# Thirteen identity matmuls put ahead of TensorE's first work, in a kernel whose order a planner writes

## The chip, the core and the metric

The kernel runs on one core of a Trainium2 chip. Its time is device time in microseconds (us), of one execution of the whole program; lower is better. Five engines run beside each other, each through its own list of instructions in the order in which they were issued: TensorE (in the profile PE for the matmuls and PEld for its weight loads), VectorE (DVE), ScalarE (ACT), GpSimd (POOL) and SyncE (SP, which here issues the DMAs). A span is the time from the first to the last instruction of one profiled execution.

## What is computed

First a chunked attention over `q`, `k`, `v` of shape (4, 8, 768, 64): each chunk of 32 queries sees 16 keys to the left, its own 32, 8 to the right, and 8 memory keys. Then a gated feed-forward network (FFN) on the 512-wide result.

```python
scores = scale * q_c @ k_full.T                 # per chunk of 32 queries
a = exp(scores - max); a = a / (sum(a) + 1e-9)
x = a @ v_full                                  # -> (4, 768, 512)

h = maximum(x @ w_in, 0)                        # 512 -> 1024
conv = cw[0]*h[t-1] + cw[1]*h[t] + cw[2]*h[t+1] # along the sequence, per channel
out = (h * 1/(1 + exp(-conv))) @ w_out          # 1024 -> 512
```

The weights `w_in`, `conv_w` and `w_out` arrive as float64. The kernel takes their 64-bit words apart on the chip and makes two single-precision parts of each (hi and lo), and it splits the activations in the same way, so each product of the FFN is three matmuls: hi·hi, hi·lo, lo·hi.

## The kernel before, in words

The attention is cut into 32 steps, numbered 0 to 31: four batches, two halves of the sequence, four pairs of heads. One step is:

- scores: 12 small matmuls on PE (L481, tile `s`);
- softmax: maximum on DVE (L397), exponential on ACT (L423 straight from the scores, or L402 on DVE and L435 on ACT), sum (L448) and reciprocal (L455) on DVE, the division on DVE or POOL (L459);
- three transposes on PE (L502, tile `t`), two copies of them on ACT into `a_d` (L513);
- 12 matmuls with the values on PE (L521, tile `a`), then the split of the result into `x_hi` on ACT (L530) and `x_lo` on DVE (L533).

The FFN takes 128 channels (one `fc` of eight) at a time. Its first layer (L556, 256 pieces of three matmuls) needs `x` of a half batch; ACT applies the ReLU (L573). The gate (L583 to L614) runs on ACT, DVE and POOL: three convolution taps (L583, L593), the sigmoid on ACT (L597), the product (L601), and the split into `g_hi` on ACT (L611) and `g_lo` (L614). The second layer (L632, 200 pieces of three matmuls) takes `g`; ACT copies the result out (L644), SP writes it. The conversions of the weights (L286 to L363) run on ACT, DVE and POOL during the first 115 us or so.

Exponential and sigmoid stand in two different function tables of ACT. Where the order goes from the one to the other, an ACT_TABLE_LOAD stands in the list of ACT.

The order of all this is not written by hand. Every piece of work is put down with `plan.op`: its engine, an assumed cost in ns, a due time from the table `DUE`, what it reads and writes, and for ACT which function table it needs. `Plan.run` then plays the whole program through with the assumed costs. At each moment it takes the engine that can start something earliest, and of what that engine could start within 1 ns the piece with the lowest due time; a piece that needs the other function table counts as 100.2 later (`SWITCH`). It also hands out the buffers: PSUM banks for `s` (2), `t` (1), `a` (1) and `f` (4, the FFN's), and the rings in SBUF. The engines' lists come out in the order in which the planner started the pieces, and on the chip each engine follows its list in that order, waiting wherever the next instruction's inputs are not there.

So the assumed cost of one piece does not only stand for itself: it sets when the planner thinks the engine is free, and with that the order of whatever comes after.

The identity (`ident`, 128x128, float32) is made at the start on POOL; the transposes use it.

Of the kernel before, what the change touches and what calls it, by code (L numbers as in the profile page):

```python
# [210 lines left out]


PAIRS = False
SWITCH, MODE = 100.2, 12.1


@with_exitstack
def attention_then_gated_ffn(
# [10 lines left out]
    nc = tc.nc  # L229
# [4 lines left out]
    P = 128  # L234
# [8 lines left out]
    plan = Plan()  # L243

    def tile_of(tag, n, shape, dtype=F32, pool=None):

        plan.ring(tag, n)
        pool = pool or work
        return Tile(tag, lambda: pool.tile(shape, dtype, name=tag, tag=tag, bufs=n))

    def bank(tag, n):
        return tile_of(tag, n, [P, 512], pool=psum)

    ident = const.tile([P, P], F32, name="ident")
# [117 lines left out]
    def attention(steps, due, soft, norm, zadd):  # L372
# [3 lines left out]
        W = 2 * NG * KW  # L376
        e = tile_of("e", 2, [P, 2, 2 * NG, KW]) if PAIRS else tile_of("e", 3, [P, 1, 2 * NG, KW])
        top, z = (tile_of(x, 4, [P, 2, 2 * NG]) for x in ("top", "z"))
# [198 lines left out]
    def gate(fc, h, due, tap, mult, keep=False):  # L577

        c = tile_of("c", 3, [P, S])
        w = [cw[:, 3 * fc + i : 3 * fc + i + 1] for i in range(3)]  # L580
        H = ((h, 0), (h, 1), "cw")
        if tap == "A":
            plan.op("A", act(S, ptr=1), due, lambda: nc.scalar.activation(c.t, h.t[:, 0:S], AF.Copy, scale=w[0]), H, (c,))  # L583
        else:
            plan.op(
                "V", vec(S, 2, 1), due,
                lambda: nc.vector.tensor_scalar(out=c.t, in0=h.t[:, 0:S], scalar1=w[0], scalar2=None, op0=ALU.mult),
                H, (c,), shared=True,
            )
        for i in (1, 2):  # L590
            plan.op(
                "V", vec(S, 1, 1), due,
                lambda i=i: nc.vector.scalar_tensor_tensor(  # L593
                    out=c.t, in0=h.t[:, i : i + S], scalar=w[i], in1=c.t, op0=ALU.mult, op1=ALU.add
                ), (*H, c), (c,), shared=True,
            )
        plan.op("A", act(S), due, lambda: nc.scalar.activation(c.t, c.t, AF.Sigmoid), (c,), (c,), table="sigmoid")  # L597
        y = (lambda: h.t[:, 1 : S + 1]) if keep else (lambda: c.t)
        plan.op(
            mult, vec(S) if mult == "V" else 2.0 * S, due,  # L600
            lambda: (nc.vector if mult == "V" else nc.gpsimd).tensor_tensor(  # L601
                out=y(), in0=c.t, in1=h.t[:, 1 : S + 1], op=ALU.mult
            ), (c, h), (h if keep else c,), shared=True,
        )
        return (h if keep else c), y
# [63 lines left out]
    def steps(i, n):  # L669

        while i < n:
            size = GROUP[i // 4] == "2" and i % 2 == 0 and 2 or 1
            attention(range(i, i + size), T_ATT[i : i + size], SOFT[i], NORM[i], ZADD[i])
            i += size

    def through_gate(b, fc, due, keep=False):
        i = b * NFC + fc
        return gate(fc, hs[b, fc][0], due, TAP[i], MULT[i], keep)

    steps(0, 4)  # L680
    for fc in range(NFC):
        convert("in", w_in[fc], w_in_p, fc, W_IN[fc], lin("w_in", fc), lin("w_in_load", fc))
# [8 lines left out]
    for fc in range(NFC):  # L691
        due = lin("gate0", fc)
        g.append(split(*through_gate(0, fc, due), due, LO[fc]))
# [4 lines left out]
    for tt in range(4, 6):  # L698
        ffn_out(0, g, tt, [lin("out0b", fc) + 0.1 * tt for fc in range(NFC)])
    y = [through_gate(1, fc, lin("gate1", fc), True) for fc in range(NFC)]  # L700
    g = [split(*y[fc], lin("split1", fc), LO[NFC + fc]) for fc in range(NFC)]
    steps(16, 24)
# [10 lines left out]
    for b in range(2, B):  # L713
        tokens_in(b, (0, 1), t, 4.2)
        g = []
        for fc in range(NFC):
            due = t + lin("gate", fc)
            g.append(split(*through_gate(b, fc, due), due, LO[b * NFC + fc]))
        if b + 1 < B:
            steps((b + 1) * NU, (b + 2) * NU)  # L720
        out_rest(b, g, t + 34, b + 1 == B)
        t += 34 + 34 + 14
# [78 lines left out]
```

## Time and profile before

| | |
|---|---|
| time, median of 3 runs | 358.87 us (358.48 to 359.29) |
| span of the profiled execution | 357.6 us |
| PE busy | 341.4 us, 95% of the span |
| DVE, ACT, POOL busy | 244.7, 240.4, 125.2 us |
| PE's first instruction | 6.8 us after the start |
| PE busy from 22.65 us to the end | 329.6 of 335.0 us |

The profiled execution is known by its span alone, 357.6 us; the median of the timed runs is 1.3 us above it, which is taken as what lies around the span. "Busy" is the time in which at least one instruction of the engine runs; instructions on PE overlap, so the durations of single ones add up to more than that.

### The profile page before, as it was taken

How to read it: one execution, taken by the hardware profiler on the slowest of the kernel's cores; microseconds unless marked ns; L12 is line 12 of the kernel's file. 1: busy time of each engine (PE TensorE's matmuls, PEld its weight loads, DVE VectorE, ACT ScalarE, POOL GpSimd, SP SyncE). 2: the span in 40 equal slices, each digit the busy share in tenths (PEclk: the TensorE clock that was granted, in tenths of full speed). 3: DMA queues.
4: the chain of work that ended last, by engine and by line, in shares of the span. 5: the costliest groups of instructions: out<-in, count | busy, mean ns of one | idle time of the engine just before them, and what ended most of it. 6: DMA issues, size and time to landing. Idle time of an engine off the chain costs nothing.

```text
span 357.6 us, 7589 instructions
## 1 busy us (share of the span) xinstructions
PE 341.4 (95%) x3000; PEld 302.1 (84%) x3000; DVE 244.7 (68%) x408; ACT 240.4 (67%) x492; POOL 125.2 (35%) x167
## 2 busy tenths in 40 slices
PE   1699999999999999999999999999999999999996
PEld 1588899999899987778888899997878799998886
DVE  3899898988889998779933026889644128998000
ACT  4468588878679999887979158877466345675101
POOL 2376554442373253774572003354010002560000
PEclk9989999999999999999999999999999999999999
DMA  7999961969623146134416200006272000000111
GB/s 267 402 387 311 383 234 63 341 208 283 209 95 116 25 139 227 68 104 152 129 44 250 88 31 0 2 0 188 80 294 75 30 31 2 0 0 3 59 59 61
DMA packets 19909, 48.63 MB, mean 136 GB/s; under 512 B 2337, under 2 KB 6689, under 8 KB 19873
## 3 DMA queue, kind: packets, MB, share of 16 engines
q1 hardware_dynamic: 19872, 48.14, 39.0%
q8 instruction: 24, 0.39, 0.5%
q14 instruction: 13, 0.10, 0.1%
HBM read 41.84 MB, written 6.29 MB: 135 GB/s over the span
## 4 chain that ended last, share of the span: by engine, by line
PE 69%; DVE 10%; DMA 5%; ACT 5%; POOL 5%; issue 4%; SPq 1%; POOLq 0%; DVEq 0%; ACTq 0%
PE f L632 33%; PE f L556 24%; PE a L521 5%; PE s L481 5%; DVE c L593 3%; PE t L502 2%; DMA h<-in_k_dram 2%; POOL c L601 2%; DMA w<-in_w_out_dram 2%; ACT c L597 2%; DMA w<-in_w_in_dram 2%; POOL w_top L293 2%; DVE z L448 1%; DVE w_top L299 1%; DVE top L397 1%
## 5 line engine op out<-in xcount | busy, mean ns | idle before, releaser
L632 PE MATMUL f<-w_out_hi,g 128*128 128x512 f32 (+1 forms) x400 | 127.6, 391 | 0.2 <-ACT o_sb L644 0.2
L556 PE MATMUL f<-x_hi,w_in_hi 128*128 128x384 f32 x256 | 88.7, 346 | 0.0
L632 PEld LDWEIGHTS f<-w_out_hi,g 128*128 128x128 f32 x400 | 74.1, 188 | 16.3 <-ACT o_sb L644 0.4
L556 PE MATMUL f<-x_hi,w_in_lo 128*128 128x384 f32 x256 | 86.2, 337 | 0.1
L556 PE MATMUL f<-x_lo,w_in_hi 128*128 128x384 f32 x256 | 86.1, 336 | 0.0
L593 DVE SCALAR_TENSOR_TENSOR c<-h,cw,c 128x768 f32<-128x768 f32 x48 | 65.9, 1380 | 27.6 <-ACT c L583 26.1
L632 PE MATMUL f<-w_out_lo,g 128*128 128x512 f32 (+1 forms) x200 | 77.0, 385 | 0.0
L556 PEld LDWEIGHTS f<-x_hi,w_in_hi 128*128 128x128 f32 x256 | 48.1, 188 | 1.2
L556 PEld LDWEIGHTS f<-x_hi,w_in_lo 128*128 128x128 f32 x256 | 48.2, 188 | 0.5 <-POOL w_in_lo L358 0.4
L556 PEld LDWEIGHTS f<-x_lo,w_in_hi 128*128 128x128 f32 x256 | 48.1, 188 | 0.0
L632 PEld LDWEIGHTS f<-w_out_lo,g 128*128 128x128 f32 x200 | 37.6, 188 | 7.2
L601 POOL TENSOR_TENSOR c<-c,h 128x768 f32<-128x768 f32 x9 | 15.8, 1752 | 70.2 <-ACT c L597 68.1
L459 POOL TENSOR_TENSOR e<-e,z 128x384 f32<-128x384 f32 x24 | 24.9, 1035 | 41.4 <-DVE z L455 27.1
L644 ACT COPY o_sb<-f 128x512 f32<-128x512 f32 (+1 forms) x25 | 14.1, 569 | 35.1 <-PE f L632 32.8
L573 ACT ACTIVATE h<-f 128x384 f32<-128x384 f32 x48 | 23.1, 492 | 17.2 <-PE f L556 16.8
L521 PEld LDWEIGHTS a<-a_d,v_t 128*64 128x64 f32 x768 | 25.7, 140 | 10.3 <-issue 5.0
L513 ACT COPY a_d<-t 64x384 f32<-64x384 f32 x64 | 30.3, 474 | 4.3 <-PE t L502 3.3
L533 DVE TENSOR_TENSOR x_lo<-a,x_hi 128x384 fp32r<-128x384 f32 x32 | 17.6, 551 | 22.3 <-ACT x_hi L530 22.2
L521 PE MATMUL a<-a_d,v_t 128*64 128x64 f32 x768 | 29.9, 229 | 1.9 <-ACT a_d L513 1.8
L597 ACT ACTIVATE c<-c 128x768 f32<-128x768 f32 x32 | 26.9, 845 | 3.8 <-DVE c L593 3.6
L530 ACT CAST x_hi<-a 128x384 fp32r<-128x384 f32 x32 | 15.4, 481 | 20.2 <-PE a L521 18.6
L423 ACT ACTIVATE e<-s,top 128x64 f32<-128x64 f32 (+3 forms) x96 | 24.4, 319 | 4.2 <-DVE top L409 2.8
(73 smaller groups left out, 479.8 us busy)
## 6 DMA issues: line engine op xcount, KB each, us to landing
v_t<-in_v_dram SPq DMA_DIRECT2D x32, 384.0 KB, 4.1
q_d<-in_q_dram SPq DMA_DIRECT2D x28, 384.0 KB, 5.1
k_t<-in_k_dram SPq DMA_DIRECT2D x28, 252.0 KB, 5.2
out_dram<-o_sb SPq DMA_DIRECT2D x23, 256.0 KB, 2.1
w<-in_w_in_dram SPq DMA_DIRECT2D x8, 512.0 KB, 5.9
w<-in_w_out_dram SPq DMA_DIRECT2D x8, 512.0 KB, 6.4
h<-in_q_dram SPq DMA_DIRECT2D x4, 384.0 KB, 7.0
h<-in_k_dram SPq DMA_DIRECT2D x4, 252.0 KB, 7.1
```

The lines of the kernel that those rows point to most:

```text
L423: nc.scalar.activation(part(e, i)[r, g, c], s_()[r, g, c], AF.Exp, bias=part(top, i)[r, g : g + 1], scale=SCALE, accum_out=part(z, i)[r, g ...
L459: lambda i=i: (nc.vector if norm == "V" else nc.gpsimd).tensor_tensor(out=part(e, i), in0=part(e, i), in1=part(z, i).unsqueeze(2).broadcas ...
L481: nc.tensor.matmul(s.t[j * D : (j + 1) * D, o : o + KW], lhsT=q_d.t[:, c], rhs=k_t.t[:, c * STEP : c * STEP + KW], start=True, stop=True,)
L513: nc.scalar.copy(out=a_d[r, :, p, :], in_=t.t[r, : NG * P].rearrange("p (g q) -> p g q", q=CH))
L521: nc.tensor.matmul(a.t[h * D : (h + 1) * D, g * P + j * D : g * P + (j + 1) * D], lhsT=v_t.t[:, g, j, h], rhs=a_d[:, 4 * g + 2 * j + h].re ...
L533: lambda: nc.vector.tensor_tensor(out=x_lo.t[:, cc], in0=a.t[:, :TW], in1=x_hi.t[:, cc].bitcast(F32), op=ALU.subtract),
L556: nc.tensor.matmul(f.t[:, :TW], lhsT=w_in_p[c][:, fc, cc], rhs=x_p[a].t[:, cc], start=(cc == 0 and i == 0), stop=(cc == NCC - 1 and i == 2),)
L573: nc.scalar.activation(h.t[:, 1 + o : 1 + o + TW], f.t[:, :TW], AF.Relu)
L593: lambda i=i: nc.vector.scalar_tensor_tensor(out=c.t, in0=h.t[:, i : i + S], scalar=w[i], in1=c.t, op0=ALU.mult, op1=ALU.add), (*H, c), (c ...
L597: plan.op("A", act(S), due, lambda: nc.scalar.activation(c.t, c.t, AF.Sigmoid), (c,), (c,), table="sigmoid")
L601: lambda: (nc.vector if mult == "V" else nc.gpsimd).tensor_tensor(out=y(), in0=c.t, in1=h.t[:, 1 : S + 1], op=ALU.mult), (c, h), (h if kee ...
L632: nc.tensor.matmul(ps.t[:, :n], lhsT=g[fc][a].t[:, tt * P : (tt + 1) * P], rhs=w_out_p[c][:, fc, o : o + n], start=(fc == 0 and i == 0), s ...
```

## The change

A constant `WARM = 13`, and one more piece of work ahead of all the others: 13 matmuls of the identity with itself, 128x128 by 128x128 in float32, into a bank of the FFN's ring `f` that nothing reads. It is put down for PE with a cost of 430 ns for each matmul, 5590 ns in all, and a due time of -1000, so the planner takes it first.

```diff
+WARM = 13
 SWITCH, MODE = 100.2, 12.1
...
+    def warm_up():
+        x = bank("f", 4)
+
+        def mm():
+            for _ in range(WARM):
+                nc.tensor.matmul(x.t[:, :P], lhsT=ident, rhs=ident, start=True, stop=True)
+
+        plan.op("PE", 430 * WARM, -1000, mm, (), (x,), mode="whole")
...
+    warm_up()
     steps(0, 4)
```

Nothing else in the text differs, and no piece of work is removed. The line numbers of the changed kernel are one higher from the constant to the function, 11 higher behind it.

The order does differ. The first place is the head of PE's list. Now:

```order
L682 MATMUL f<-ident 128x128 x13
L482 MATMUL s<-h 64x64 x48
L503 MATMUL t<-ident,e 128x128 x3
L522 MATMUL a<-a_d,v_t 64x64 x12
L503 MATMUL t<-ident,e 128x128 x3
L482 MATMUL s<-k_t,q_d 64x64 x12
L522 MATMUL a<-a_d,v_t 64x64 x12
```

Behind the 13 matmuls stand the same rows as before, the scores of steps 0 to 3 (x48) first. The lists of all engines go on unchanged for some time, PE's for 30 rows, DVE's for 45, ACT's for 23, POOL's for 25, SP's for 30; from there on they differ in many places.

The second place is the list of ACT between the exponential of step 12 and that of step 13. Before (the three rows of L423 are the exponential of step 13; `w_out_hi` is a converted weight, `c` and `g` belong to the gate and the FFN):

```order
L423 ACTIVATE e<-s,top 128x64 x6
L573 ACTIVATE g<-f 128x384 x3
L312 CAST w_out_hi<-w_top 128x512
L583 ACTIVATE c<-g,cw 128x768
L423 ACTIVATE e,z<-s,top 128x64 x5
L423 ACTIVATE e,z<-s,top 64x64
L423 ACTIVATE e,z<-s,top 64x56
L530 CAST x_hi_1111<-a 128x384
```

Now:

```order
L424 ACTIVATE e<-s,top 128x64 x6
L574 ACTIVATE g<-f 128x384 x3
L313 CAST w_out_hi<-w_top 128x512
L584 ACTIVATE c<-g,cw 128x768
L598 ACT_TABLE_LOAD
L598 ACTIVATE c<-c 128x768
L290 ACTIVATE w_top<-w_1055 128x512
L531 CAST x_hi_1118<-a 128x384
L574 ACTIVATE g<-f 128x384 x2
L612 CAST g<-c 128x768
```

A load of the sigmoid's table and a first sigmoid (L598) have come in where the exponential of step 13 stood. That exponential comes 33 rows further on, behind a load of the other table:

```order
L584 ACTIVATE c<-g,cw 128x768 x2
L313 CAST w_out_hi<-w_top 128x512
L574 ACTIVATE h<-f 128x384
L424 ACT_TABLE_LOAD
L424 ACTIVATE e,z<-s,top 128x64 x5
L424 ACTIVATE e,z<-s,top 64x64
L424 ACTIVATE e,z<-s,top 64x56
```

Before, ACT loaded no sigmoid table ahead of the exponentials of steps 13 to 16; now it does so once and loads the exponential's table back. The whole list has 18 table loads before and 18 now.

The third place is PE's list at the transposes of step 16. Now:

```order
L557 MATMUL f<-x_lo_1340,w_in_hi 128x384
L482 MATMUL s<-k_t,q_d 64x64 x24
L522 MATMUL a<-a_d,v_t 64x64 x12
L557 MATMUL f<-x_hi_1321,w_in_hi 128x384
L557 MATMUL f<-x_hi_1321,w_in_lo 128x384
L557 MATMUL f<-x_lo_1340,w_in_hi 128x384
L503 MATMUL t<-ident,e 128x128 x3
```

Here the scores of two steps (x24) and the values of step 15 stand close ahead of the transposes of step 16. Counted from the start of the list, 17 steps of scores and 106 pieces of the FFN's first layer stood ahead of these transposes before, and 20 steps of scores and 103 pieces do now; ahead of the values of step 16 it was 17 and 109, and is 20 and 108.

On DVE's list, ahead of the reciprocal of step 16, there are now two more multiply-adds of the gate (L593), two more products (L601) and one more split (L614) than before, and eight shorter instructions trade places, four for four. On ACT's list, ahead of the copies of `a_d` for step 16, there are now one exponential (L435), two first taps (L583), a sigmoid (L597), two casts of `g_hi` (L611) and two table loads more, and one ReLU (L573) less.

## The prediction

> **What bounds the kernel now.** I read the page's head and its chain first, then PE's busy time by stretches.
>
> ```profile
> span 357.6 us, 7589 instructions
> PE 341.4 (95%) x3000; PEld 302.1 (84%) x3000; DVE 244.7 (68%) x408; ACT 240.4 (67%) x492; POOL 125.2 (35%) x167
> PE 69%; DVE 10%; DMA 5%; ACT 5%; POOL 5%; issue 4%; SPq 1%; POOLq 0%; DVEq 0%; ACTq 0%
> ...
> 0.00:22.65 22.65, 11.72 (x178) 10.45 (x179) 15.61 (x39) 11.21 (x23) 9.72 (x17) 0.92 0.94 348
> 22.65:357.60 334.95, 329.63 (x2823) 291.63 (x2822) 229.06 (x370) 229.18 (x469) 115.50 (x151) 1.00 0.36 122
> 60.00:111.00 51.00, 50.23 (x549) 46.87 (x549) 44.55 (x87) 42.22 (x116) 21.14 (x39) 1.00 0.61 199
> ```
>
> In the stretches the columns are the length, then busy time of PE, PEld, DVE, ACT and POOL, then the granted clock. PE sets the end: from 22.65 us on it is idle for 334.95 - 329.63 = 5.3 us in all. PE's work is fixed, so an idle microsecond that is added there is added to the end, and one taken away at the start is taken away at the end, as long as its inputs keep up. Whether they do is read from 60 to 111 us: DVE is busy 44.55 and ACT 42.22 of 51 us, so those two can't fall far behind the order they have now.
>
> At the start, in order of time:
>
> ```profile
> 0.99 0.29 POOL masks.py:199 TENSOR_SCALAR_AFFINE_SELECT ident<-ident 128x128 f32<-128x128 f32 x1
> 6.82 1.55 PE L481 MATMUL s<-h 128*64 128x64 f32 x24 [6.82 <-DMA h<-in_k_dram]
> 8.41 0.56 DVE L397 TENSOR_REDUCE top<-s 128x6 f32<-128x384 f32 x1 [0.62 <-PE s L481]
> 10.09 4.77 PE L481 MATMUL s<-h 128*64 128x64 f32 x72 [1.72 <-DMA h<-in_k_dram]
> 14.90 0.75 PE L502 MATMUL t<-ident,e 128*128 128x128 f32 x3
> 17.48 0.92 PE L521 MATMUL a<-a_d,v_t 128*64 128x64 f32 x24 [1.82 <-ACT a_d L513]
> 19.27 1.55 PE L481 MATMUL s<-k_t,q_d 128*64 128x64 f32 x24 [0.40 <-DVE z L448]
> 20.58 1.52 PE L521 MATMUL a<-a_d,v_t 128*64 128x64 f32 x24
> 22.39 0.42 PE L556 MATMUL f<-x_hi,w_in_hi 128*128 128x384 f32 x1
> ...
> 18.00:19.00 1.00, 0.87 (x17) 0.56 (x13) 0.64 (x4) 0.98 (x3) 0.86 (x2) 0.89 1.06 401
> 19.00:20.00 1.00, 0.73 (x14) 0.76 (x16) 1.00 (x3) 0.95 (x4) 1.00 (x2) 0.50 1.08 405
> 22.00:23.00 1.00, 1.00 (x8) 0.81 (x6) 0.97 (x3) 0.75 (x2) 1.00 (x2) 0.90 1.02 403
> ```
>
> The scores of a step (x24) take 1.55 us where PE is slow; 24 matmuls of that shape take 0.92 us at 17.48. The slow ones at 19.27 and 20.58 coincide with a granted clock of 0.50. That from 6.82 the column shows 1.00 beside the same 1.55 us I take for a missing first record: PE starts at half clock.
>
> **The change, part by part.**
>
> *The thirteen matmuls.* They can start when the identity is there, at 0.99 + 0.29 = 1.28 us. PE's first work waits for its DMA until 6.82, and that wait is their cover. The trace has no plain float32 matmul of this shape. The scores are 12 in the program and 24 in the trace, so I count 26. Upper bound by the three transposes at 14.90, same shape at half clock: 26 x 0.25 = 6.5 us, end at 7.8, which is 1.0 late. Lower bound by the scores, half the columns: 26 x 0.065 = 1.7 us, end at 3.0. I take the end before 6.82: the clock should rise on the way. If the cover fails, step 0's scores end at 7.8 + 0.92 = 8.7 instead of 8.37: a loss of 0.3. Nobody waits for the bank that they write but later matmuls on PE itself.
>
> *A faster clock at the start.* Step 0's scores would end at 6.82 + 0.92 = 7.74 instead of 8.37, 0.63 us earlier, and DVE waited 0.62 us for them. Step 1's scores wait for their own DMA until 10.09 whatever the clock; if it holds, they too end 0.63 earlier. The scores and values at 19.27 and 20.58 could lose 0.6 us each. So the gain is at most 0.6 + 1.2 = 1.8 us and at least the loss of 0.3, if the clock falls again in the pause from 7.74 to 10.09. In the trace it did fall to 0.50 after a pause of 1.82 us (before 17.48). Since DVE is nearly full by then (1.00 and 0.97 of the last two rows), I take 0.5 us.
>
> [...]
>
> *The order.* This is the larger part. The planner keeps PE taken for 5.59 us more at the start, and from about the thirtieth row on all lists differ. What matters is the stretch before 111 us, where a sigmoid now stands ahead of the exponential of step 13. I compare what each engine must do before step 16, because there the trace shows almost no room:
>
> ```profile
> 107.56 0.82 POOL L459 TENSOR_TENSOR e<-e,z 128x384 f32<-128x384 f32 x1
> 108.49 0.50 PE L502 MATMUL t<-ident,e 128*128 128x128 f32 x3
> 109.61 0.95 ACT L513 COPY a_d<-t 64x384 f32<-64x384 f32 x2
> 110.61 0.49 PEld L521 LDWEIGHTS a<-a_d,v_t 128*64 128x64 f32 x14 [0.37 <-ACT a_d L513]
> ```
>
> The softmax ends at 108.38 and the transposes start at 108.49: 0.11 us of room. The copies end at 110.56, the values start at 110.61: 0.05. Prices, from the groups by form (busy, mean ns of one) and two pieces of the chain (start, us):
>
> ```profile
> L593 DVE SCALAR_TENSOR_TENSOR c<-g,cw,c 128x768 f32<-128x768 f32 x16 | 18.0, 1132 | 0.9 <-ACT c L583 0.8
> L601 DVE TENSOR_TENSOR c<-c,g 128x768 f32<-128x768 f32 x3 | 2.8, 951 | 0.0
> L614 DVE TENSOR_TENSOR g<-c,g 128x768 fp32r<-128x768 f32 x16 | 16.1, 1005 | 2.6 <-ACT g L611 2.5
> L597 ACT ACTIVATE c<-c 128x768 f32<-128x768 f32 x32 | 26.9, 845 | 3.8 <-DVE c L593 3.6
> L597 ACT ACT_TABLE_LOAD x9 | 11.5, 1283 | 0.1
> L583 ACT ACTIVATE c<-g,cw 128x768 f32<-128x768 f32 x8 | 7.5, 933 | 0.0
> L611 ACT CAST g<-c 128x768 fp32r<-128x768 f32 x24 | 20.0, 832 | 7.2 <-DVE c L601 4.4 <-POOL h L544 1.3 <-POOL c L601 1.2
> L435 ACT ACTIVATE e<-e 128x384 f32<-128x384 f32 x17 | 8.8, 522 | 2.9 <-DVE e L441 2.7
> L573 ACT ACTIVATE h<-f 128x384 f32<-128x384 f32 x48 | 23.1, 492 | 17.2 <-PE f L556 16.8
> ...
> 46.72 0.70 PE s L481 x24
> 112.23 10.10 PE f L556 x57
> ```
>
> So a step's scores cost PE 0.70 us and an FFN piece of three matmuls 10.10 / 19 = 0.53.
>
> - DVE, ahead of the reciprocal of step 16: 2 x 1.13 + 2 x 0.95 + 1.01 = 5.2 us more (of the eight short instructions that trade places four go and four come; counted as nothing). PE, ahead of the transposes: three scores more and three pieces less, 3 x 0.70 - 3 x 0.53 = 0.5. PE waits 5.2 - 0.5 - 0.1 = 4.6 us.
> - ACT, ahead of the copies: 0.52 + 2 x 0.93 + 2 x 1.28 + 0.85 + 2 x 0.83 - 0.49 = 7.0 us more. PE, ahead of the values: 3 x 0.70 - 0.53 = 1.6. PE waits 7.0 - 1.6 - 0.05 = 5.4 us.
>
> These two are one wait, not two: what delays the softmax delays the copies. It shrinks by what idle time DVE and ACT can fill, since PE is then the one that waits:
>
> ```profile
> DVE w L315 <- DMA w<-in_w_out_dram: 1.9, 1, 1.9
> DVE top L397 <- PE s L481: 1.4, 2, 0.9
> ...
> ACT x_hi L530 <- PE a L521: 1.7, 3, 0.8
> ACT g L573 <- PE f L556: 1.2, 3, 0.6
> ACT x_hi L530 <- PE f L556: 1.0, 1, 1.0
> ```
>
> These are waits between 60 and 111 us. Without its waits for PE, DVE's sum falls to 4.6 - 1.4 = 3.2, without the DMA's too to 1.3; ACT's falls to 5.4 - 3.9 = 1.5. Lower bound of the stall 1.3; upper bound 5.4, and 6.6 if the clock drops once on the way, as at 19.27 and 20.58 (0.6 us on each). I take 4.0, between 3.2 and 5.4: the wait for DMA has its own cause and may stay. Then steps 17 to 20 run with what they are given, and from step 21 on both orders have done nearly the same work, so nothing is added and nothing is won back: PE has no idle time left to fill.
>
> [...]
>
> *Sum*, against the profiled execution: 357.6 - 0.5 + 4.0 = 361.1 us of span, and 1.3 us around it (the median of the runs is 358.87): **362.4 us**. With the bounds together: 357.6 - 1.8 + 1.3 + 1.3 = 358.4, and 357.6 + 0.3 + 6.6 + 1.3 = 365.8.
>
> **The rivals.**
>
> *The start wins (0.16).* The clock holds through the pauses, 1.8 us are won, and DVE and ACT fill nearly all their idle time, which leaves 0.5 us of stall: 357.6 - 1.8 + 0.5 + 1.3 = 357.6 us. For it: the waits for PE between 60 and 111 us. Against it: DVE is 87% busy there, and its waits for PE are only 1.4 us. It decides from the point where the stall is below 1.8.
>
> *Even (0.08).* A gain of 1.3 against the lowest stall of 1.3: 358.9 us. That the matmuls do not raise the clock at all (they may count for less than full ones) belongs on the other side: no gain, 362.9, inside the forecast.
>
> *Worse (0.06).* The waits at steps 13 to 16 come apart and the clock drops at three of them, 1.2 us each: 357.6 + 5.4 + 3.6 + 1.3 = 367.9 us. For it: the fall after a pause of 1.82 us. Against it: between the waits PE still has FFN pieces.
>
> **How the numbers follow.** The forecast, 362.4, has a chance of 0.70, with a range of its own of 358.4 to 365.8. For all, I give 357.6 to 367.0. That leaves out the worst case and the better half of the first rival. A difference of under 0.2% (0.7 us) can't be told from none here. Slower by more than that: 0.70 + 0.06, less 0.02 for the forecast's low end, 0.74; within it 0.08 + 0.02 = 0.10; faster 0.16.
>
> **What would show it.** In the changed profile: 26 matmuls on `ident` from 1.3 us on; step 0's scores at 6.8 in about 0.92 us; PE's first FFN matmul less than 1.8 us before 22.39. Between 75 and 115 us PE idles some 4 us ahead of L503 and L522, released by POOL, ACT or DVE, with a table load in ACT's list just before. Behind 130 us the stretches look as now. I am wrong if PE's idle time there is under 1.8 us, or if most of the added time lies elsewhere: at the start, in slower matmuls, or behind 200 us.

## The result and the profile after

The changed kernel takes 364.44 us (median of 4 runs, 363.91 to 364.81), the kernel before 359.08 us (4 runs, 358.48 to 360.31) beside it: a ratio of 1.0122, 95% interval 1.0081 to 1.0162. It is slower, by 1.2% or some 4.4 us; the two medians lie 5.4 us apart, which is inside that interval too. The forecast was 362.4 us with a range of 357.6 to 367.0. The profiled execution took 363.91 us with a span of 362.1, so 1.8 us lie around the span instead of the 1.3 that I had added. No run with a span on record has less than 1.7 there, so the 1.3 was too small from the start.

The head of the page, and the stretches that the prediction showed of before (length, then busy time of PE, PEld, DVE, ACT, POOL, then the granted clock, the share of the DMA engines and GB/s):

```profile
span 362.1 us, 7634 instructions
PE 346.4 (96%) x3026; PEld 307.5 (85%) x3026; DVE 246.5 (68%) x408; ACT 240.3 (66%) x492; POOL 126.2 (35%) x167
...
22.65:362.10 339.45, 332.24 (x2836) 294.64 (x2832) 231.10 (x370) 229.52 (x470) 115.60 (x149) 0.99 0.35 120
60.00:111.00 51.00, 48.59 (x540) 45.18 (x540) 47.99 (x91) 44.57 (x117) 23.44 (x38) 0.97 0.60 201
```

From 60 to 111 us PE is idle for 2.41 us instead of 0.77, DVE has risen from 44.55 to 47.99 us of 51, and the granted clock has fallen from 1.00 to 0.97. Two places carry the loss. The first is the start (PE's list in order of time; the last columns are the idle time ahead and what ended it):

```profile
1.34 5.84 PE L682 MATMUL f<-ident 128*128 128x128 f32 x26 [1.34 <-POOL ident masks.py:199]
7.12 0.92 PE L482 MATMUL s<-h 128*64 128x64 f32 x24
9.48 0.92 PE L482 MATMUL s<-h 128*64 128x64 f32 x24 [1.45 <-DMA h<-in_k_dram]
...
16.46 0.94 PE L522 MATMUL a<-a_d,v_t 128*64 128x64 f32 x24 [2.03 <-ACT a_d L514]
...
20.30 1.55 PE L482 MATMUL s<-k_t,q_d 128*64 128x64 f32 x24 [2.06 <-DMA k_t<-in_k_dram]
21.61 1.52 PE L522 MATMUL a<-a_d,v_t 128*64 128x64 f32 x24
...
23.61 0.62 PE L557 MATMUL f<-x_hi,w_in_hi 128*128 128x384 f32 x1
```

The 26 matmuls run from 1.34 to 7.18 us, 0.22 us each, so the cover up to 6.82 just fails to hold. The scores of steps 0 to 3 then run in 0.92 us instead of 1.55, and the values of step 0 start 1.02 us earlier than before (16.46 against 17.48). That lead is lost in the wait of 2.06 us for the keys of step 4: its scores start at 20.30, before at 19.27. From there to the first FFN matmul PE runs at half rate (granted clock 0.50 from 17.22 to 24.05 us) and takes 3.31 us; before it took 3.12, at half rate for most of it too (0.50 from 18.78 to 22.19). So the first FFN matmul comes 1.22 us later (23.61 against 22.39), 1.03 of it ahead of step 4's scores. The keys' load was issued earlier than before (11.96 against 12.55); why it landed later is not shown.

The second place is the stretch around 100 us, on five engines (SPq are the DMAs that SP issues):

```profile
94.77 1.28 ACT L424 ACT_TABLE_LOAD   x1
96.06 0.31 ACT L424 ACTIVATE e<-s,top 128x64 f32<-128x64 f32 x1
98.57 0.92 PE L482 MATMUL s<-k_t,q_d 128*64 128x64 f32 x24
99.33 0.18 DVE L456 RECIPROCAL z<-z 128x6 f32<-128x6 f32 x1
99.66 0.83 POOL L460 TENSOR_TENSOR e<-e,z 128x384 f32<-128x384 f32 x1 [1.00 <-DVE z L456]
99.75 0.92 PE L482 MATMUL s<-k_t,q_d 128*64 128x64 f32 x24 [0.26 <-ACT e L424]
99.90 0.43 SPq L472 DMA_DIRECT2D k_t<-in_k_dram  x1
100.60 0.55 PE L503 MATMUL t<-ident,e 128*128 128x128 f32 x3
101.81 0.98 ACT L514 COPY a_d<-t 64x384 f32<-64x384 f32 x2
103.25 1.55 PE L482 MATMUL s<-k_t,q_d 128*64 128x64 f32 x24 [2.10 <-DMA k_t<-in_k_dram]
104.55 1.52 PE L522 MATMUL a<-a_d,v_t 128*64 128x64 f32 x24
```

The exponential of step 13 starts at 96.06, behind a table load. In the kernel before it stood here:

```profile
69.28 0.31 ACT L423 ACTIVATE e<-s,top 128x64 f32<-128x64 f32 x1
```

From 98.57 on PE has only attention in its list, the scores of steps 15, 16 and 17 and step 13's transposes and values; its next FFN matmul comes at 106.31. It waits 2.10 us for the keys of step 17, whose load was issued at 99.90, when step 15's scores had given the buffer back, and in that pause the granted clock falls to half: it is 0.50 from 102.55 to 105.97.

Counted by stretches, idle time of PE before and after: 0.72 and 0.34 us from 24 to 45; 0.77 and 2.41 from 85 to 115; none and 0.36 from 115 to 135; 0.49 and 0.17 from 135 to 260; none and 0.58 from 260 to 285. With the 1.22 us of the start that is 3.1 us of the 4.5 by which the span grew. The other 1.4 are what is left over. Half rate between 85 and 115 us, where the mean clock is 0.94, accounts for most of it: the scores at 103.25 and the values at 104.55 take 1.55 and 1.52 us instead of 0.92 each, 1.2 us more.

### The profile page after: what moved, and what is told of

It reads as the page before. It is cut to its first block, busy times and chain, and to the rows that moved or that the text cites. A ratio compares the mean times of both kernels' runs of the same rounds, so it can differ in the third digit from the quotient of the medians.

```text
span 362.1 us, 7634 instructions
## 1 busy us (share of the span) xinstructions
PE 346.4 (96%) x3026; PEld 307.5 (85%) x3026; DVE 246.5 (68%) x408; ACT 240.3 (66%) x492; POOL 126.2 (35%) x167
## 5 line engine op out<-in xcount | busy, mean ns | idle before, releaser
L522 PEld LDWEIGHTS a<-a_d,v_t 128*64 128x64 f32 x768 | 26.3, 143 | 8.2 <-issue 3.8
L522 PE MATMUL a<-a_d,v_t 128*64 128x64 f32 x768 | 30.4, 231 | 2.0 <-ACT a_d L514 2.0
L482 PE MATMUL s<-k_t,q_d 128*64 128x64 f32 x672 | 25.5, 230 | 4.8 <-DMA k_t<-in_k_dram 4.2
L482 PEld LDWEIGHTS s<-k_t,q_d 128*64 128x64 f32 x672 | 22.8, 144 | 8.2 <-ACT a_d L514 2.6
```

What stands on the lines that cost most here:

```text
L482: nc.tensor.matmul(s.t[j * D : (j + 1) * D, o : o + KW], lhsT=q_d.t[:, c], rhs=k_t.t[:, c * STEP : c * STEP + KW], start=True, stop=True,)
L522: nc.tensor.matmul(a.t[h * D : (h + 1) * D, g * P + j * D : g * P + (j + 1) * D], lhsT=v_t.t[:, g, j, h], rhs=a_d[:, 4 * g + 2 * j + h].re ...
```

## The experiments

All ratios are to the kernel before, run beside each kernel on the same chip, and the medians of before there were 359.7 to 360.2 us. Where a kernel keeps an order, "the order of before" or "the changed order" means every row of every engine's list, but for the rows that its edit names.

**The two halves apart.** The matmuls with the order of before, by telling the planner that they are free:

```diff
-        plan.op("PE", 430 * WARM, -1000, mm, (), (x,), mode="whole")
+        plan.op("PE", 0, -1000, mm, (), (x,), mode="whole")
```

> The thirteen matmuls run, but the planner is given a cost of 0 for them, so every engine's list is as before apart from the new first piece of PE. Theory A (the order is what costs): between 357.5 and 359.5 us, that is within 1.5 us of before; the clock at the start gives at most 1.8 us. Theory B (the matmuls themselves cost: they hold PE or shift the clock at the start): 360.5 us or more, with PE's first FFN matmul later than in the kernel before (22.4 us) by about as much.

The changed order without the matmuls:

```diff
-            for _ in range(WARM):
+            for _ in range(0):
```

> The order of the changed kernel (the planner still counts 5.59 us), but no matmul on the identity is issued. Theory A: 363.5 to 365.5 us, as the changed kernel. Theory B: 358 to 360 us, as before. If the two effects add up, this run and the one with the matmuls alone together give the 5.4 us.

The matmuls alone: 361.44 us, ratio 1.0037 (1.0010 to 1.0064). The order alone: 363.40 us, ratio 1.0078 (1.0048 to 1.0108). Together 1.15%, and the whole change costs 1.22%. So both halves lose, the order about two thirds; each theory had given the whole loss to one of them. Measured against the profiled execution of before, the first FFN matmul of the matmuls alone stands 0.84 us later, pieces 24 to 72 of the first layer 0.95 later and the last pieces 1.30 later: what is lost at the start is never won back.

Single profiles scatter at the start. In the order alone, which has no opening matmuls, the first FFN matmul stands at 23.16. Over the profiles with the same list of PE up to there it stands at 21.95 to 23.16 without any added matmuls (five profiles) and at 23.23 to 24.08 with the thirteen alone (three). So the thirteen do move it, but the 0.84 and the 1.22 us are each known only roughly.

**A third order, and the table loads.** The planner counts 6000 ns instead of 5590:

```diff
-        plan.op("PE", 430 * WARM, -1000, mm, (), (x,), mode="whole")
+        plan.op("PE", 6000, -1000, mm, (), (x,), mode="whole")
```

> The same thirteen matmuls, but the planner counts 6.0 us for them instead of 5.59, which gives a third order, as far from the changed one as that is from before. If the loss belongs to this one order's misfortune (the sigmoid ahead of step 13), another order may land anywhere; if any order other than the one before loses here, 361 us or more. I expect 361 to 367 us.

And the changed kernel with two sigmoids replaced by a plain copy (that part of the gate is left out), so that ACT needs no table load ahead of step 13's exponential and none for it (`gate` takes the function as its last argument):

```diff
-        return gate(fc, hs[b, fc][0], due, TAP[i], MULT[i], keep)
+        return gate(fc, hs[b, fc][0], due, TAP[i], MULT[i], keep, AF.Copy if b == 0 and fc < 2 else AF.Sigmoid)
```

> The changed kernel, order kept, but the sigmoid of the first two channel groups of batch 0 is replaced by a copy of the same size on ScalarE, which leaves that part of the gate out; the two table loads ahead of step 13's and step 17's exponentials disappear with it. If ScalarE's late softmax of steps 13 to 16 is the bound (my sum: two loads of 1.28 us in it), the time falls by 1.3 to 2.6 us to 361.8 to 363.1. If VectorE's extra work or the load of k_t sets the wait, it falls by under 0.7 us.

6000 ns: 361.70 us, ratio 1.0035 (1.0011 to 1.0059), not to be told from the matmuls alone; no cost of that order shows. It has two sigmoids ahead of step 13's exponential too, at 71.13 and 80.90, but the exponential starts at 93.20, 2.9 us earlier, and PE still has FFN pieces between the steps: it idles 0.54 us from 85 to 115. So in this order a late exponential costs nothing that can be seen; for the stall the FFN pieces have to run out as well.

Without the two loads: 365.31 us, ratio 1.0126 (1.0086 to 1.0166), no gain that can be told. PE idles 2.72 us from 85 to 115 (2.41 in the changed kernel) and waits at the same place:

```profile
97.98 1.34 ACT L424 ACTIVATE e<-s,top 128x64 f32<-128x64 f32 x6
99.61 1.62 PE L482 MATMUL s<-k_t,q_d 128*64 128x64 f32 x48
100.41 0.18 DVE L456 RECIPROCAL z<-z 128x6 f32<-128x6 f32 x1
104.49 0.97 PE L482 MATMUL s<-k_t,q_d 128*64 128x64 f32 x24 [2.32 <-DVE e L444]
```

Step 13's exponential is over when step 14's starts, at 97.98, but DVE comes to its reciprocal only at 100.41: some 2 us lie in DVE's own list. The profile of the changed kernel says the same: from 85 us up to that reciprocal, at 99.33, DVE works without a wait, so an earlier exponential alone could not have brought it forward. Of my two estimates of the stall the one by ACT, with its 2 x 1.28 us of loads, falls. The times alone would not decide it: the half rate at the start lasted longer in this profile (granted clock 0.50 from 9.64 to 26.70, 17.06 us), and its first FFN matmul stands at 24.08.

**Is it the load of step 17?** The page of the changed kernel names a DMA. In the changed order without the matmuls, step 17 takes its queries and keys from step 16 and its own are left out. Pieces 818 and 819 are the two loads, 821 and 803 the scores of steps 17 and 16:

```diff
+            if i in (818, 819):
+                continue
...
+                    x.t = ops[803][5][("q_d", "k_t").index(x.ring)].t if i == 821 and x.ring in ("q_d", "k_t") else x.make()
```

> The order that the change gives, without its matmuls, and step 17's queries and keys are not loaded: its scores are made from those of step 16, so that this load is left out and its attention is not that of the reference. Theory A (the load of step 17 ends the wait of 2.3 us at 103.55 us, since its buffer comes free only with step 15's scores): that wait goes; next, TensorE waits for ScalarE's copies of step 13, which ended at 102.9 us, so that the gain is 1.0 to 1.4 us: span 360.2 to 360.6, ratio to before 1.004. Rival B (the softmax of steps 13 to 15 sets the stretch, as I predicted, and the load only ends first): idle time of TensorE between 85 and 115 us stays above 3.2 us (3.63 with the load), span 361.2 to 361.8, ratio 1.008.

365.77 us, ratio 1.0124 (1.0076 to 1.0173): no faster than the order alone, and not surely slower, since the intervals overlap and the six runs fall into 362.6 to 363.6 and 365.7 to 366.2. Of the order alone the profile has these rows:

```profile
103.55 0.92 PE L482 MATMUL s<-k_t,q_d 128*64 128x64 f32 x24 [2.28 <-DVE e L444]
104.26 0.90 PE L522 MATMUL a<-a_d,v_t 128*64 128x64 f32 x24
```

Here the page names DVE for the wait that it put down to the DMA in the changed kernel. Without the load that wait is shorter, and others take its place:

```profile
PE f L564 <- DVE x_lo L541: 1.7, 1, 1.7
PE s L489 <- ACT e L431: 1.2, 2, 0.9
PE f L564 <- ACT h L581: 0.4, 1, 0.4
...
102.60 0.92 PE L489 MATMUL s<-k_t,q_d 128*64 128x64 f32 x24 [0.91 <-ACT e L431]
103.43 0.92 PE L529 MATMUL a<-a_d,v_t 128*64 128x64 f32 x24
108.07 0.51 PE L564 MATMUL f<-x_lo,w_in_hi 128*128 128x384 f32 x1 [1.67 <-DVE x_lo L541]
```

Step 17's scores come at 102.60 instead of 103.55, step 13's values at 103.43 instead of 104.26, and then PE waits 1.67 us for `x_lo` of DVE (1.08 with the load). It idles 3.27 us from 85 to 115 (3.63 with the load), above the 3.2 of rival B, and the mean granted clock is 0.94 there, against 1.00 in the profiled execution with the load. The load can end the wait, but without it the softmax and DVE hold nearly all of the idle time.

**Undoing the planner's decision.** The changed order's root is one choice: a sigmoid ahead of step 13's exponential, after which the exponential counts 100.2 later. One rule more, with the matmuls left out and their 5590 ns kept:

```diff
-        plan.op("A", act(S), due, <sigmoid>, (c,), (c,), table="sigmoid")
+        plan.op("A", act(S), due, <sigmoid>, (c, ("exps", 13)), (c,), table="sigmoid")
```

where the exponential of step n writes `("exps", n)` and `<sigmoid>` stands for a call that is the same in both lines; and the same with steps 13 to 16.

> No matmuls of the identity, the planner still counts 5590 ns for them, and one rule more: a sigmoid of the gates may only be planned behind the exponential of step 13. Theory A (that exponential, put behind two sigmoids, is what delays steps 13 to 17 and lets TensorE run out of FFN matmuls): idle time of TensorE between 85 and 115 us falls from 3.63 us to at most 1.2 us (0.77 before), span 358.2 to 359.4, ratio to before 0.999 to 1.003. Rival B (any order but the tuned one has such a place): TensorE idles 3 us or more in that stretch or in another one, span 361 to 362, ratio 1.007 to 1.010.

> No matmuls of the identity, the planner still counts 5590 ns for them, and the sigmoids of the gates may only be planned behind the exponentials of steps 13, 14, 15 and 16. Theory A (an exponential that the planner puts behind sigmoids is what holds up the attention steps there; with step 13 alone set free the same happened to step 14 at 102.50 us): no exponential of steps 13 to 16 stands behind a sigmoid, TensorE idles at most 1.2 us between 85 and 115 us (3.63 with the changed order, 2.68 with step 13 alone set free, 0.77 before), span 357.5 to 359.0, ratio to before 0.996 to 1.001. Rival B (any order but the one before has about 3 us of such waits somewhere): ratio 1.006 to 1.010, with the idle time at another place, for instance at the gates behind 115 us, whose sigmoids now come later.

Step 13 alone: 364.39 us, ratio 1.0113 (1.0074 to 1.0151), no better than the order alone. ACT's rows tell why:

```profile
78.69 1.28 ACT L598 ACT_TABLE_LOAD   x1
79.99 0.85 ACT L598 ACTIVATE c<-c 128x768 f32<-128x768 f32 x1
...
101.21 1.28 ACT L424 ACT_TABLE_LOAD   x1
102.50 2.57 ACT L424 ACTIVATE e<-s,top 128x64 f32<-128x64 f32 x12
```

Step 13's exponential now runs at 70.48, but the sigmoids come next and the same has happened to steps 14 and 15 (x12 at 102.50).

With the rule for steps 13 to 16: 361.25 us, ratio 1.0035 (1.0010 to 1.0060), between the two theories. But the rule does not reach step 16. The gates of the first batch are put down ahead of step 16, and a piece waits only for what was put down before it. So the exponentials of steps 13 to 15 come ahead of all sigmoids (69.73, 80.80, 84.39), as in the kernel before, while that of step 16 stands behind 16 sigmoids, and its transposes with it:

```profile
170.43 1.33 ACT L424 ACTIVATE e<-s,top 128x64 f32<-128x64 f32 x6
...
176.20 0.49 PE L503 MATMUL t<-ident,e 128*128 128x128 f32 x3
```

Before, these transposes ran at 108.49. This order also has 6 table loads instead of 18. The stretch from 85 to 115 us, in this order: before, the changed order alone, step 13 set free, steps 13 to 15 set free with step 16 put off:

```profile
85.00:115.00 30.00, 29.23 (x301) 27.53 (x302) 26.19 (x47) 24.98 (x54) 12.99 (x25) 1.00 0.51 163
```

```profile
85.00:115.00 30.00, 26.37 (x325) 24.30 (x324) 28.73 (x56) 26.96 (x69) 16.19 (x25) 1.00 0.56 180
```

```profile
85.00:115.00 30.00, 27.32 (x295) 24.71 (x295) 28.40 (x52) 25.94 (x60) 14.48 (x28) 1.00 0.51 164
```

```profile
85.00:115.00 30.00, 30.00 (x270) 28.89 (x269) 26.12 (x43) 25.10 (x50) 11.11 (x25) 1.00 0.39 124
```

PE's idle time there goes 0.77, 3.63, 2.68, 0.00. With the exponentials of steps 13 to 15 ahead of the sigmoids the stall is gone altogether, and DVE has 26.12 us to do instead of 28.73. Since step 16's softmax has left the stretch as well, this run alone does not show which of the two did it. The kernel before helps: there steps 13 to 15 are early, step 16's exponential stands in the stretch (100.95), and PE idles only 0.77 us. And in all six traces in which the exponentials of steps 14 and 15 come after 97 us and PE's list then has attention alone for 4 us or more, PE idles 2.4 to 3.7 us. That supports the late exponentials as the cause; no run moves them and nothing else. The time does not come down to that of before: the first FFN matmul stands 0.44 us earlier (21.95), the last piece of the first layer 1.30 later (321.32 against 320.02). From 115 to 250 us PE idles 1.29 us instead of 0.20, in waits of at most 0.5 us; this is another order there, with the rest of the attention put off, and what else takes time I did not find.

**The start.** Four kernels keep the order of before and change only what runs in the first 20 us. Six matmuls instead of thirteen:

```diff
-WARM = 13
+WARM = 6
...
-        plan.op("PE", 430 * WARM, -1000, mm, (), (x,), mode="whole")
+        plan.op("PE", 0, -1000, mm, (), (x,), mode="whole")
```

> Six matmuls of the identity instead of thirteen, and the planner counts them as free, so that the order of all other work is that of the kernel before. At 0.22 us a pass they end near 4.0 us, 2.8 us ahead of the first scores. Theory A (the thirteen cost 1.3 us because they move the stretch at full rate: the scores of steps 0 to 3 run fast, and the half rate then falls on 17 to 24 us, where TensorE sets the pace): after a pause of 2.8 us the first scores run in 1.55 us as before, the first FFN matmul stands at 22.4 us (within 0.5), span 357.6 to 358.2, ratio to before 1.000. Rival B (what costs is that matmuls stand there at all, whatever the rate does): about 6/13 of 1.3 us, span 358.2, ratio 1.002, with the first FFN matmul at 22.8 us or later.

360.39 us, ratio 1.0009 (0.9982 to 1.0036); first FFN matmul at 22.40 us. No difference that can be told, as theory A had it; the 1.002 of rival B lies in the interval too, but its first FFN matmul at 22.8 us or later does not come. Only theory A's step on the way was wrong: step 0's scores ran in 0.92 us after a pause of 3.05 us, and steps 1 to 3 at half rate (granted clock 0.50 from 8.20 to 15.03).

Thirteen, and 24 more in the pauses behind the first scores, the first and the second transposes (the table counts PE's pieces):

```diff
+KEEP = {1: 6, 2: 2, 3: 2, 5: 8, 7: 6}
...
+            if e == "PE":
+                for _ in range(KEEP.get(n, 0)):
+                    self.fill()
+                n += 1
```

> Thirteen matmuls of the identity at the start, the order of the kernel before, and 24 more of them in the pauses of TensorE behind the first scores (6, 2, 2), the first transposes (8) and the second transposes (6), so that no pause of the first 20 us is longer than about 0.7 us. Theory A (the cost of the start is the rate): the granted clock stays at 1.00 up to 25 us, step 4's scores and the values of steps 0 and 1 take 0.92 us instead of 1.55, the first FFN matmul stands at 21.7 to 22.0 us (13 alone: 23.23; before: 22.39), span 357.0 to 357.9, ratio to before 0.996 to 1.000. Rival B (the loads and the softmax set the start, whatever the rate): step 4's scores still wait for their load until about 19.9 us and the first FFN matmul comes later than 22.5 us; span 358.5 to 359.0, ratio 1.003.

359.43 us against 360.05, ratio 0.9967 (0.9941 to 0.9994): faster than before, as theory A had it, and span 357.0.

```profile
16.36 0.92 PE L533 MATMUL a<-a_d,v_t 128*64 128x64 f32 x24 [0.24 <-ACT a_d L525]
19.52 0.92 PE L493 MATMUL s<-k_t,q_d 128*64 128x64 f32 x24 [0.42 <-DVE x_lo L545]
20.23 0.90 PE L533 MATMUL a<-a_d,v_t 128*64 128x64 f32 x24
21.37 0.42 PE L568 MATMUL f<-x_hi,w_in_hi 128*128 128x384 f32 x1
```

The first FFN matmul stands at 21.37 us, 1.86 us ahead of the thirteen alone and 1.02 ahead of before; 0.6 of that is left at the end, since ahead of 48 us PE waits for others again.

No opening matmuls, five behind the first transposes and three behind the second (`KEEP = {5: 5, 7: 3}`, `range(0)`); and the thirteen with eight and six there, none between the scores (`KEEP = {5: 8, 7: 6}`):

> The order of the kernel before, no matmuls ahead of step 0, and eight matmuls of the identity later: five behind the first transposes, three behind the second ones. Theory A (what costs at the start is the half rate from 17 to 24 us alone): TensorE is busy nearly without a pause from 10.1 us on, step 4's scores and step 1's values run in 0.92 us, the first FFN matmul stands at 21.4 to 22.0 us, span 356.8 to 357.6, ratio 0.995 to 0.998, as with the thirteen and 24 more (0.9967). Rival B (the opening matmuls are needed too, since without them the rate is still half when these eight run, and at half rate they take 0.44 us each and push the values of step 0 back): first FFN matmul at 22.4 us or later, span 357.6 to 358.5, ratio 0.999 to 1.002.

> The order of the kernel before, thirteen matmuls of the identity at the start, and fourteen more in two pauses alone: eight behind the first transposes, six behind the second ones (the pauses between the scores of steps 0 to 3 stay). Theory A (only the pause of 2.03 us ahead of step 0's values and the next one bring the half rate back; the shorter ones between the scores do not): the granted clock stays at 1.00 to 25 us, the first FFN matmul stands at 21.2 to 21.8 us (21.37 with all 24; 23.23 with none), span 356.8 to 357.5, ratio to before 0.995 to 0.999. Rival B (the pauses of 1.5 to 2 us between the scores of steps 0 and 1 are enough for the half rate, as in two other runs where it came at about 10 and 11 us): first FFN matmul at 22.0 us or later, span 357.8 to 359.0, ratio 0.999 to 1.003.

The first: 359.78 us, ratio 1.0006 (0.9989 to 1.0024), the first FFN matmul at 21.75 us, as theory A had it, and the time as rival B had it; behind the scores of steps 0 to 3 no row shows half rate (the mean granted clock of the profiled execution is 0.998). The second: 359.36 us, ratio 0.9991 (0.9969 to 1.0013), first FFN matmul at 22.29 us. Neither can be told from before. In the second the half rate did come back between the scores (steps 1 to 3 took 4.16 us, 1.39 each, against 0.92 for step 0's), as its rival B had it. So a gain was measured only with both, the opening and the filled pauses, and its interval only just leaves out 1 and overlaps those of these two: that both are needed is not shown.

**Both together.** The changed kernel with the 24 more:

> The changed kernel as it is, with its order and its thirteen matmuls, and 24 more of them in the pauses of the start (6, 2, 2, 8, 6). Theory A (the loss is a sum of two parts, the half rate at the start and the stall at steps 13 to 17 that the new order brings): the start's part goes and the stall stays, so that the first FFN matmul stands at 21.3 to 21.9 us (23.61 without the 24), and TensorE still idles 2.7 to 3.7 us between 85 and 115 us; span 359.8 to 361.2, ratio to before 1.005 to 1.009 (1.0122 without the 24). Rival B (the stall absorbs what the start gains, since ScalarE and VectorE set the pace up to there): first FFN matmul as early, but span 361.5 to 362.5 and ratio 1.010 to 1.014.

363.38 us, ratio 1.0092 (1.0055 to 1.0129), first FFN matmul at 22.15 us, PE idle 3.66 us from 85 to 115.

```profile
20.30 0.92 PE L493 MATMUL s<-k_t,q_d 128*64 128x64 f32 x24 [1.26 <-DMA k_t<-in_k_dram]
...
22.15 0.42 PE L568 MATMUL f<-x_hi,w_in_hi 128*128 128x384 f32 x1
```

Step 4's scores wait for their keys until 20.30, as in the changed kernel, but from there to the FFN it is 1.85 us at a granted clock of 1.00, instead of 3.31 at 0.50. In the stall PE waits 3.40 us for the keys of step 17 (2.10 in the changed kernel), so the load's share differs from one execution to the next. The start's part shrinks and the stall stays, between the two theories: 1.0122 and 1.0092 have overlapping intervals, so the sum of two parts is supported and not shown.

## Why the prediction was right, and where it was not

*The direction and the main step held.* "The order. This is the larger part": 0.78 of 1.22%. The place (between 75 and 115 us), the sign, and the cause (a sigmoid ahead of step 13's exponential, so that the softmax and what hangs on it are late) are supported by the four rows above. The size, 4.0 us, was too large for the order alone: idle time there grew by 2.86 us in the profile of the order alone, and the runs say 2.8. In the changed kernel it is 1.64 us of idle time and about 1.4 of half rate, 3.0 in all.

*Part of the hit is luck.* My sign of being wrong was that "most of the added time lies elsewhere: at the start, in slower matmuls, or behind 200 us". In the changed kernel it does: of 4.5 us of span, 1.64 are idle time between 75 and 115 us, 1.22 lie at the start, about 1.4 in slower matmuls and 0.58 at 274 us. In the order alone the sign does not come: 2.86 of 4.0 us are idle time there. So the mechanism holds for the order. The total came as near as 2.0 us in part because the 1.7 us missed at the start and the 1.0 us too much at the stall pull against each other.

*How the stall was argued was half right.* I compared sums of work at step 16. The stall comes at step 13 to 17, where PE's stock of FFN pieces has run out; ACT's sum (5.4) was not the bound, DVE's (4.6) was the nearer one, and taking out the 2 x 1.28 us of table loads brought no gain that could be told. I had said that PE would wait ahead of L503 and L522; it waited ahead of L482, for a load that itself waited for a late step. "Behind 130 us the stretches look as now" failed by 0.6 us, a wait ahead of transposes at 274 us, which the order alone does not show.

*The start failed, with its sign.* "I take 0.5 us" of gain; the matmuls alone cost 1.3 us. It is the step "A faster clock at the start". I asked whether the clock holds from one pause to the next and priced single pauses; how long the half rate lasts, and how much PE works ahead of it, I had not looked at. Three stretches of before and four of after, each as long as the half rate in before, 18.78 to 22.19 us, and counted from where the clock changes:

```profile
11.95:15.37 3.42, 3.28 (x50) 2.94 (x48) 3.12 (x12) 0.64 (x2) 1.09 (x2) 1.00 1.04 401
15.37:18.78 3.41, 1.59 (x30) 1.12 (x28) 2.83 (x11) 3.34 (x11) 2.52 (x4) 1.00 1.04 398
18.78:22.19 3.41, 3.01 (x50) 2.83 (x50) 3.36 (x7) 1.80 (x5) 3.25 (x4) 0.50 1.04 399
```

```profile
10.39:13.81 3.42, 1.85 (x49) 1.62 (x48) 3.23 (x10) 0.52 (x1) 0.81 (x1) 1.00 1.05 401
13.81:17.22 3.41, 1.31 (x27) 1.07 (x27) 2.85 (x10) 2.94 (x10) 2.34 (x5) 1.00 1.02 393
17.22:20.63 3.41, 1.34 (x15) 0.88 (x13) 3.25 (x8) 2.34 (x5) 3.17 (x5) 0.50 1.04 398
20.63:24.05 3.42, 3.42 (x52) 3.30 (x49) 1.58 (x4) 0.48 (x1) 1.90 (x2) 0.50 0.97 344
```

Before, the scores at half rate (72 in 4.77 us) and the transposes keep PE busy for 3.28 us of the first stretch, and by 17.48 the full rate is there (24 matmuls in 0.92); the second is 1.59 busy, and then the clock is 0.50 for one stretch, which is 3.01 busy, up to 22.19. After, the scores take 0.92 us a step instead of 1.55, so PE has less to do: 1.31 busy up to 17.22, and the clock is 0.50 from there; it is 0.50 through the next two, 1.34 and 3.42 busy, and 1.00 again from 24.05. The matmuls bought speed where the loads set the pace (9.48 <- DMA, 20.30 <- DMA), and the half rate still stands where PE does. It is two stretches of half rate instead of one, and they end 1.86 us later. Much of the first one falls on the wait for step 4's keys, which is the other part of the loss and which I had not priced.

*The rivals.* "The start wins" would have been 357.6: it needed a start that gains, and only the run with all pauses filled had one. "Even" and "Worse" were not met. *The sum* was 362.4 for 364.4. In the span 1.7 us were missing at the start (1.2 lost where 0.5 was to be won), 1.0 too much stood at the stall (3.0 instead of 4.0), 0.6 was missed at 274 us and 0.3 too much in the rest: 362.1 for 361.1. Another 0.5 lies around the span, and 0.5 is what the median stands above the profiled execution.

## What to carry to other kernels

Filling TensorE once at the start did not keep its rate here: behind the thirteen matmuls the granted clock was 0.50 from 17.22 to 24.05 us. So look at the clock and the durations up to the point where TensorE becomes the bound. The opening alone cost time (ratio 1.0037), and with the later pauses filled too the gain was 0.3%. Where a planner's costs set the order, a piece of work that costs nothing by itself can still cost most by its number: put it in with a cost that leaves the lists as they are, and compare the lists. And when the profile names a DMA as what ended a wait, see when that DMA could be issued before blaming it: here its removal won nothing that could be told.

## What the runs showed of the hardware

The granted clock read 0.50 in these stretches: in the kernel before from 18.78 to 22.19 us (3.41 us); in the changed kernel from 17.22 to 24.05 (6.83) and from 102.55 to 105.97 (3.42); with the matmuls alone from 17.14 to 23.97 (6.83); with six from 8.20 to 15.03 (6.83) and from 18.44 to 21.85 (3.41); with step 13 set free from 17.72 to 21.13, and with the rule for steps 13 to 16 from 17.92 to 21.33 (3.41 each); with 6000 ns from 11.40 to 21.64 (10.24); without the table loads from 9.64 to 26.70 (17.06).

TensorE's busy time in the 3.41 us ahead of these falls, in the same order: 1.59; 1.31 and 1.74; 1.32; 0.88 and 1.36; 1.13; 1.36; 1.40; 1.52 us. In stretches of the same length at a granted clock of 1.00, with 1.00 behind them too, it was 1.96 and 1.85 in the changed kernel (6.98 to 13.81) and 2.34 to 3.27 with all pauses filled (7.00 to 20.64). In the 3.41 us ahead of the rises that end the half rate in the first 30 us it was 3.01 in the kernel before and 3.25 to 3.42 elsewhere; within the half rate it was 1.34 in the changed kernel, 1.72 with the matmuls alone, 1.40 with six, 2.62 and 2.30 with 6000 ns and 2.21 to 2.83 without the table loads, and the clock stayed at 0.50. These are the rows of this case; what sets the clock they do not show.

In the kernel before the granted clock reads 1.00 from 6.82 to 8.37 us, beside scores that take 1.55 us as they do at 0.50 (19.27): there the durations tell the rate, the column does not.
